# Output transform of a row-wise Winograd ResBlock: two-bank pairs through ScalarE to bf16, instead of f32 arithmetic on PSUM

## The chip, the cores and the metric

The kernel runs on one core of a Trainium2 chip. The metric is the device time of one execution in microseconds. The kernel before took 568.13, 567.94 and 566.29 us in three runs: median 567.94. One further execution was taken with the hardware profiler; every start and duration below is from it. The engines are TensorE (PE, with its weight loads as PEld), VectorE (DVE), ScalarE (ACT), GpSimd (POOL) and SyncE (SP), whose queue here issues nearly all DMA transfers. "L628" is line 628 of the kernel.

## The reference

The kernel computes one ResBlock of a diffusion model on bf16 tensors: batch 2, 512 channels, 64 x 64 pixels, four channel groups.

```
h = conv3(silu(gn(x, g1, be1)), w1)            # 3x3, padding 1
h = h + (silu(t_emb) @ w_emb).reshape(B, C, 1, 1)
h = conv3(silu(gn(h, g2, be2)), w2)
return x + h
# gn: per group of 128 channels: (z - mean) / sqrt(var + 1e-5) * gamma + beta
```

A channel group has 128 channels, which is just one tile of 128 partitions. The statistics of GroupNorm for a group need the sum and the sum of squares over a whole tile of 128 x 4096 values.

## The kernel before

**The convolution.** Each 3x3 convolution is done in a Winograd form along rows: four output rows are made from six transformed input rows. The six are called positions, 0 to 5. For each position, TensorE adds up products over 4 input channel tiles and 3 horizontal taps, so 12 matmuls of 128x128 weights by 512 columns (L628) fill one PSUM bank (128 x 512 f32). Six positions make a *set*: 72 matmuls, which give 32 output rows of 128 output channels. A *chunk* is one half image (32 rows) of one batch element, and has four sets, one for each output channel tile `ot`. There are four chunks in a layer and two layers: 32 sets and 2304 such matmuls.

**Around the matmuls, per set.** `evac(pos)` (L632 to L702) is called behind the matmuls of each position, in the order 1, 2, 3, 4, 0, 5. ScalarE copies positions 1 and 3 from PSUM to f32 tiles c1 and c3 with a factor 1/6 (L635, L649). VectorE combines positions 2 and 4 with them in f32, reading PSUM (L642, L654), so that t1 = p1 + p2 and t2 = p3 + p4 (scaled), and gets s1 = p1 - p2 and s2 = p3 - p4 by a multiply and subtract (L644, L656). The four output rows are then y1 = s1 + 2 s2, y2 = t1 + 4 t2, y0 = p0 + t1 + t2, y3 = p5 + s1 + 8 s2. In layer 0 (L661 to L667, L685, L693) four of these products also add up their own sums for the second GroupNorm, ScalarE squares the finished rows for the sum of squares (L697) into its own tile `junk`, and a DMA stores them to the scratch tensor h_scr (L699). In layer 1 (L669 to L681, L689, L701) the residual x, loaded as `xr`, is added by four more VectorE additions, and the result goes out (L702). There are 10 such VectorE operations per set in layer 0 and 14 in layer 1, each on 128 x 512 values with f32 on at least one side. PSUM holds six single-bank accumulators (pool `ps_acc`), and two further banks (`ps_x`) serve small products and transposes.

**Work beside it.** Three kinds of background tasks feed the matmuls:

- `produce_V` (L386) makes the transformed input V of the next chunk. For each of 4 input tiles: one load (from x in layer 0, from h_scr in layer 1), one ScalarE Silu with the GroupNorm's scale and bias (L415), and 14 VectorE operations in bf16 (L454 to L472). For the very first chunk, ScalarE does part of the scalings (L434 to L444).
- `prep_U` (L288) makes the transformed weights U of one output and one input tile: load of the weights (L290), nine TensorE transposes (L299, L302), two ScalarE copies from PSUM (L303, L305), and six VectorE operations (L328 to L336), of which three are fused multiply-adds through an f32 tile (L333, L334, L336). It runs 32 times; U of layer 0 is kept for both batch elements.
- `gn1_stats_bg` (L240) gets the first GroupNorm's statistics of batch element 1 while batch element 0 is convolved: for each of four channel tiles two loads (L245) into the pool `stg` under the tag "xr" (two buffers), ScalarE passes for the sum (L212) and the sum of squares (L216), and `gn_scale_bias` (L161): one small TensorE product over the partitions (L163), VectorE steps (L165 to L171, L180, L181) and two GpSimd steps (vare L173, rstd L178).

**What sets the order.** The class `_Background` (L19) keeps the tasks sorted by due time and counts in slots, one slot to a position. At each `bg.tick()` it adds credit at the highest rate that any due time needs, and runs a step of the most urgent task for each whole credit. In `evac`'s loop a tick comes before `evac(pos)`; in the very first set, whose matmuls go input tile by input tile as V comes in, it comes after. The order so written is then rearranged for each engine by the framework's scheduler, and every engine works its own list in order. The x loads of the statistics and of the residual are held back until the first set's first copy has been done (`first_evac`).

Of the kernel before, what the change touches and what calls it, by code (L numbers as in the profile page):

```python
# [10 lines left out]
ALU = mybir.AluOpType  # L11
# [52 lines left out]
def kernel(  # L64
# [32 lines left out]
    FAST_U = "s"  # L97
    ACT_TS0 = True
    N_SUM_ACT = 1
    RES_ON_PE = False  # L100
# [13 lines left out]
    otmp = ctx.enter_context(tc.tile_pool(name="otmp", bufs=1))  # L114
# [3 lines left out]
    ps_acc = ctx.enter_context(tc.tile_pool(name="ps_acc", bufs=6, space=PSUM))  # L118
# [169 lines left out]
    def prep_U(layer, ot, ct, eng=None, dep=None):  # L288
# [15 lines left out]
        g1t = wtmp.tile([P, NKX, P], BF16, tag="g1t")  # L304
        nc.scalar.copy(out=g1t[:], in_=pb[:])  # L305
        g0 = U[:, :, 0, :]
        g2 = U[:, :, NPOS - 1, :]
        if FAST_U == "both":
            g0q = wtmp.tile([P, NKX, P], BF16, tag="g0q")
            nc.scalar.activation(out=g0q[:], in_=pa[:, :, 0, :], func=ACT.Copy, scale=0.25)  # L310
            g1h = wtmp.tile([P, NKX, P], BF16, tag="g1h")
            nc.scalar.activation(out=g1h[:], in_=pb[:], func=ACT.Copy, scale=0.5)
            yield
            sb_ = wtmp.tile([P, NKX, P], BF16, tag="sb")
            nc.vector.tensor_tensor(out=sb_[:], in0=g0, in1=g2, op=ALU.add)
            nc.vector.tensor_tensor(out=U[:, :, 1, :], in0=sb_[:], in1=g1t[:], op=ALU.add)
            nc.vector.tensor_tensor(out=U[:, :, 2, :], in0=sb_[:], in1=g1t[:], op=ALU.subtract)
            yield
            cb_ = wtmp.tile([P, NKX, P], BF16, tag="sb")
            nc.vector.tensor_tensor(out=cb_[:], in0=g0q[:], in1=g2, op=ALU.add)  # L320
            nc.vector.tensor_tensor(out=U[:, :, 3, :], in0=cb_[:], in1=g1h[:], op=ALU.add)
            nc.vector.tensor_tensor(out=U[:, :, 4, :], in0=cb_[:], in1=g1h[:], op=ALU.subtract)
            yield
            return
        if FAST_U == "s":
            yield
            sb_ = wtmp.tile([P, NKX, P], BF16, tag="sb")
            nc.vector.tensor_tensor(out=sb_[:], in0=g0, in1=g2, op=ALU.add)  # L328
            nc.vector.tensor_tensor(out=U[:, :, 1, :], in0=sb_[:], in1=g1t[:], op=ALU.add)  # L329
# [28 lines left out]
    def emb_task():  # L358
# [5 lines left out]
        for i in range(EMB_NP):  # L364
# [13 lines left out]
            else:  # L378
                nc.vector.tensor_tensor(out=emb_sb[:], in0=emb_sb[:], in1=ps_e[:], op=ALU.add)
            yield  # L380

    POS_ORDER = (1, 2, 3, 4, 0, 5)
    Vt = {}
    V_STEPS = 3 * CT

# [377 lines left out]
```

## Time and profile before

| what | value |
|---|---|
| three runs | 568.13, 567.94, 566.29 us |
| profiled execution, span of its instructions | 564.7 us |
| profiled execution's own time, with what lies around the span | not shown on its page |
| TensorE busy | 540.7 us (96%) |
| VectorE busy | 479.8 us (85%) |
| ScalarE busy | 218.3 us (39%) |
| TensorE clock granted | 1.00 up to the last matmul |
| first main matmul starts, last one ends | 26.3 us, 558.7 us |

The same by stages, in us busy:

| stretch | what runs in it | TensorE | VectorE | ScalarE |
|---|---|---|---|---|
| 0 to 26.3 | loads, first statistics, first weights | 17.57 | 13.83 | 15.57 |
| 26.3 to 47.5 | first set | 17.48 | 18.55 | 19.37 |
| 47.5 to 101.1 | rest of the first chunk | 53.43 | 53.60 | 53.45 |
| 101.1 to 170 | second chunk | 65.87 | 64.47 | 28.65 |
| 170 to 266 | chunks 3 and 4, in part | 96.00 | 81.01 | 35.23 |
| 266 to 346.6 | end of layer 0, entry to layer 1 | 78.28 | 70.76 | 30.29 |
| 346.6 to 558.7 | layer 1 | 212.09 | 175.23 | 35.73 |
| 558.7 to 564.7 | tail | 0 | 2.30 | 0 |

How to read what follows. A group's row names line, engine, operation, output and inputs with their shape, then total busy time and the mean duration of one instruction in ns, then the idle time of the engine just before such instructions and what ended it. A row of the timeline has start and duration in us; idle time before it stands in brackets, with its releaser. A row of waits has total, number and longest. Neighbouring instructions of one engine overlap a little in the records, so the distance from start to start is shorter than the duration: a VectorE operation on 128 x 512 f32 values lasts 0.68 us and comes every 0.605 us.

### The profile page before, as it was taken

What the parts mean: (1) busy time and instruction counts of PE and PEld (TensorE: products, weight loads), DVE (VectorE), ACT (ScalarE), POOL (GpSimd) and SP (SyncE); (2) the same over time, 40 slices, a digit from 0 to 9 for tenths busy, and PEclk for the clock granted to TensorE, in tenths of its full rate; (3) what the DMA queues carried; (4) which work ended last, traced back from release to release, by engine and by line L of the source; (5) the groups of instructions that cost most, each with busy time, mean ns of one, the idle gap of its engine ahead of it and who ended that gap; (6) DMA issues with size and microseconds to landing.
All of it is one profiled execution on the core that took longest, in us unless ns stands there. A gap on an engine that the chain in (4) does not pass through costs nothing.

```text
span 564.7 us, 7699 instructions
## 1 busy us (share of the span) xinstructions
PE 540.7 (96%) x2814; PEld 259.3 (46%) x2814; DVE 479.8 (85%) x1226; ACT 218.3 (39%) x252; POOL 23.3 (4%) x74
## 2 busy tenths in 40 slices
PE   4879999899999999999999989999999999999995
PEld 4535544344444444444445545444444444444442
DVE  2889999989988884898879999999999998555665
ACT  5699999463435332343235314322230300000000
POOL 1110000011001100000000011000000000000000
PEclk9999999999999999999999999999999999999999
DMA  8506654333523120132133512323433122222210
GB/s 336 207 22 216 192 176 139 137 114 124 161 76 108 56 105 37 45 127 96 42 101 102 160 37 76 112 80 123 153 102 101 47 75 74 75 74 76 74 39 37
DMA packets 18754, 59.83 MB, mean 106 GB/s; under 512 B 2075, under 2 KB 3227, under 8 KB 18331
## 3 DMA queue, kind: packets, MB, share of 16 engines
q1 hardware_dynamic: 18656, 59.32, 31.5%
q8 instruction: 22, 0.36, 0.3%
q14 instruction: 17, 0.14, 0.1%
q10 hardware_dynamic: 59, 0.01, 0.0%
HBM read 42.54 MB, written 16.78 MB: 105 GB/s over the span
## 4 chain that ended last, share of the span: by engine, by line
PE 72%; DVE 21%; issue 2%; DMA 2%; ACT 1%; POOL 1%; SPq 0%; DVEq 0%; ACTq 0%
PE acc L628 70%; DVE U L336 2%; DVE U L334 2%; DVE U L329 1%; DMA xbuf<-in_x_dram 1%; DVE U L330 1%; POOL rstd L178 1%; DVE cc L333 1%; PE pa L299 1%; ACT V_146 L212 1%; DMA wn<-in_w_dram 1%; DVE vq L455 1%; DVE yst L662 1%; DVE tt L666 1%; DVE ss L667 0%
## 5 line engine op out<-in xcount | busy, mean ns | idle before, releaser
L628 PE MATMUL acc<-V,U 128*128 128x512 bf16 x2016 | 444.9, 381 | 2.6 <-DVE V L457 1.6
L628 PEld LDWEIGHTS <-U 128*128 128x128 bf16 x2304 | 224.0, 98 | 273.4 <-issue 7.0
L628 PE MATMUL acc<-V_146,U 128*128 128x512 bf16 x288 | 66.4, 381 | 3.2 <-DVE V_146 L448 3.1
L697 ACT ACTIVATE junk<-yst 128x2048 bf16<-128x2048 bf16 x16 | 30.5, 1909 | 58.5 <-DVE yst L693 53.2
L303 ACT COPY U<-pa 128x768 bf16<-128x768 bf16 x32 | 25.7, 803 | 41.1 <-PE pa L299 41.1
L415 ACT ACTIVATE a_tmp_105<-src,nb_all,sc_all 128x2112 bf16<-128x2112 bf16 x14 | 30.1, 2152 | 22.2 <-DVE V L470 18.9
L415 ACT ACTIVATE a_tmp_106<-src,nb_all,sc_all 128x2112 bf16<-128x2112 bf16 x14 | 30.1, 2151 | 21.5 <-DVE vq L455 10.4
L299 PEld LDWEIGHTS <-wn 128*128 128x128 bf16 x192 | 16.5, 142 | 8.0 <-issue 2.9
L299 PE MATMUL pa<-ident,wn 128*128 128x128 bf16 x192 | 16.9, 225 | 2.6 <-DVE tot L165 2.3
L334 DVE SCALAR_TENSOR_TENSOR U<-g1t,cc 128x384 bf16<-128x384 bf16 x32 | 17.5, 546 | 0.0
L333 DVE SCALAR_TENSOR_TENSOR cc<-U 128x384 f32<-128x384 bf16 x32 | 17.5, 546 | 0.0
L336 DVE SCALAR_TENSOR_TENSOR U<-g1t,cc 128x384 bf16<-128x384 bf16 x32 | 17.5, 546 | 0.0
L305 ACT COPY g1t<-pb 128x384 bf16<-128x384 bf16 x32 | 15.8, 495 | 0.4 <-DVE U L336 0.4
L216 ACT ACTIVATE xt<-xt 128x2048 bf16<-128x2048 bf16 x8 | 15.4, 1928 | 0.1
L212 ACT ACTIVATE xt<-xt 128x2048 bf16<-128x2048 bf16 x8 | 15.4, 1928 | 0.0
L199 PE MATMUL gr<-xbuf 128*128 128x128 bf16 x96 | 7.5, 243 | 6.5 <-DMA xbuf<-in_x_dram 6.5
L693 DVE SCALAR_TENSOR_TENSOR yst<-acc,ss 128x512 bf16<-128x512 f32 x16 | 10.9, 682 | 2.5 <-PE acc L628 2.5
L457 DVE TENSOR_TENSOR V<-vq 128x528 bf16<-128x528 bf16 x28 | 11.8, 422 | 0.0
L472 DVE TENSOR_TENSOR V<-V,vq 128x528 bf16<-128x528 bf16 x28 | 11.8, 421 | 0.0
L464 DVE TENSOR_TENSOR V<-vs,vq 128x528 bf16<-128x528 bf16 x28 | 11.8, 421 | 0.0
L466 DVE TENSOR_TENSOR V<-vs,vq 128x528 bf16<-128x528 bf16 x28 | 11.8, 421 | 0.0
L469 DVE TENSOR_TENSOR V<-V,vq 128x528 bf16<-128x528 bf16 x28 | 11.8, 421 | 0.0
(660 smaller groups left out, 594.6 us busy)
## 6 DMA issues: line engine op xcount, KB each, us to landing
wn<-in_w_dram SPq DMA_DIRECT2D x32, 288.0 KB, 3.1
src<-h_scr SPq DMA_DIRECT2D x16, 528.0 KB, 3.9
h_scr<-yst SPq DMA_DIRECT2D x16, 512.0 KB, 2.6
xr<-in_x_dram SPq DMA_DIRECT2D x16, 512.0 KB, 4.1
out_dram<-yst SPq DMA_DIRECT2D x16, 512.0 KB, 3.6
src<-in_x_dram SPq DMA_DIRECT2D x12, 528.0 KB, 4.5
xt<-in_x_dram SPq DMA_DIRECT2D x8, 512.0 KB, 3.7
xbuf<-in_x_dram SPq DMA_DIRECT2D x3, 1024.0 KB, 6.2
```

The source lines that it names most:

```text
L212: nc.scalar.activation(out=o, in_=pc, func=ACT.Identity, accum_out=part[:, k:k + 1])
L216: nc.scalar.activation(out=pc, in_=pc, func=ACT.Square, scale=float(HW) ** -0.5, accum_out=part[:, k:k + 1])
L299: nc.tensor.transpose(pa[:, kx, j, :], wn_v[:, kx, 2 * j, :], ident[:])
L303: nc.scalar.copy(out=U[:, :, 0:NPOS:NPOS - 1, :], in_=pa[:])
L305: nc.scalar.copy(out=g1t[:], in_=pb[:])
L333: nc.vector.scalar_tensor_tensor(out=cc[:], in0=g0, scalar=0.25, in1=g2, op0=ALU.mult, op1=ALU.add)
L334: nc.vector.scalar_tensor_tensor(out=U[:, :, 3, :], in0=g1t[:], scalar=0.5, in1=cc[:], op0=ALU.mult, op1=ALU.add)
L336: nc.vector.scalar_tensor_tensor(out=U[:, :, 4, :], in0=g1t[:], scalar=-0.5, in1=cc[:], op0=ALU.mult, op1=ALU.add)
L415: nc.scalar.activation(out=at[:, a_ - r0:b_ - r0, 1:W + 1], in_=ap, func=ACT.Silu, bias=nb_all[:, layer, b, ct:ct + 1], scale=sc_all[:, la ...
L457: nc.vector.tensor_tensor(out=Vc[:, 1], in0=p_, in1=q, op=ALU.add)
L628: nc.tensor.matmul(accs[pos][:], lhsT=U[ct][:, kx, pos, :], rhs=V[:, ct, pos, :, kx:kx + W], start=first, stop=last)
L697: nc.scalar.activation(out=junk[:], in_=yf, func=ACT.Square, scale=float(HW) ** -0.5, accum_out=ssq[:, ch:ch + 1])
```

## The change

The order of positions becomes 1, 3, 2, 4, 0, 5, and the accumulators are taken as three pairs, (1,3), (2,4) and (0,5), each one tile over two PSUM banks. `evac` runs once for a pair. ScalarE copies a whole pair (1024 values a partition) to a bf16 tile in one instruction; the pair (0,5) only in layer 1. VectorE then forms t1, t2 in one bf16 addition of 1024 values and s1, s2 in one subtraction, and the sums for y0 and y3 in one more. The fused multiply-adds for y1 and y2 in layer 1 become a scaling and an addition; the residual is added to the four rows at once, 2048 values, at the very end. In layer 0 the pair (0,5) is still read from PSUM by VectorE. The Square pass is put off to the first copy of the next set (`pending`, `flush_stats`), and its output goes to the tag "xr" that the statistics' loads also use. The temporaries have two buffers instead of one. `prep_U` goes from six VectorE operations to eight, all in bf16. In the first set two ticks come before each `evac`.

```diff
-    otmp = ctx.enter_context(tc.tile_pool(name="otmp", bufs=1))
+    otmp = ctx.enter_context(tc.tile_pool(name="otmp", bufs=2))
+    wpool = ctx.enter_context(tc.tile_pool(name="W", bufs=1))
-    ps_acc = ctx.enter_context(tc.tile_pool(name="ps_acc", bufs=6, space=PSUM))
+    ps_acc = ctx.enter_context(tc.tile_pool(name="ps_acc", bufs=3, space=PSUM))
...
-            cc = wtmp.tile([P, NKX, P], F32, tag="sc")
-            nc.vector.scalar_tensor_tensor(out=cc[:], in0=g0, scalar=0.25, in1=g2, op0=ALU.mult, op1=ALU.add)
-            nc.vector.scalar_tensor_tensor(out=U[:, :, 3, :], in0=g1t[:], scalar=0.5, in1=cc[:],
-                                           op0=ALU.mult, op1=ALU.add)
-            nc.vector.scalar_tensor_tensor(out=U[:, :, 4, :], in0=g1t[:], scalar=-0.5, in1=cc[:],
-                                           op0=ALU.mult, op1=ALU.add)
+        nc.vector.tensor_scalar(out=g1t[:, 1], in0=g1t[:, 0], scalar1=0.5, scalar2=None, op0=ALU.mult)
+        nc.vector.tensor_scalar(out=ev[:, 0], in0=g0, scalar1=0.25, scalar2=None, op0=ALU.mult)
+        nc.vector.tensor_tensor(out=ev[:, 1], in0=ev[:, 0], in1=g2, op=ALU.add)
+        nc.vector.tensor_tensor(out=U[:, :, 3, :], in0=ev[:, 1], in1=g1t[:, 1], op=ALU.add)
+        nc.vector.tensor_tensor(out=U[:, :, 4, :], in0=ev[:, 1], in1=g1t[:, 1], op=ALU.subtract)
...
-    POS_ORDER = (1, 2, 3, 4, 0, 5)
+    POS_ORDER = (1, 3, 2, 4, 0, 5)
...
+    pending = []
+
+    def flush_stats():
+        while pending:
+            yf, sq = pending.pop(0)
+            junk = stg.tile([P, CR * W], BF16, tag="xr")
+            nc.scalar.activation(out=junk[:], in_=yf, func=ACT.Square, scale=float(HW) ** -0.5, accum_out=sq)
...
                 def evac(pos):
+                    src = pairs[pos]
+                    if pos != 0 or layer == 1:
+                        m = otmp.tile([P, 2, TR, W], BF16, tag=f"m{pos}")
+                        i_a = nc.scalar.activation(out=m[:], in_=src[:], func=ACT.Copy,
+                                                   scale=KAPPA if pos != 0 else 1.0)
...
+                    if pos == 1:
+                        flush_stats()
                     elif pos == 2:
+                        w_ = wpool.tile([P, 2, 2, TR, W], BF16, tag="w")
+                        nc.vector.tensor_tensor(out=w_[:, :, 0], in0=tmp[1][:], in1=m[:], op=ALU.add)
+                        nc.vector.tensor_tensor(out=w_[:, :, 1], in0=tmp[1][:], in1=m[:], op=ALU.subtract)
+                        t1, s1, t2, s2 = w_[:, 0, 0], w_[:, 0, 1], w_[:, 1, 0], w_[:, 1, 1]
                         if layer == 0:
+                            nc.vector.scalar_tensor_tensor(out=y4[:, 1], in0=s2, scalar=2.0, in1=s1,
+                                                           op0=ALU.mult, op1=ALU.add, accum_out=acc_sum(0))
+                            nc.vector.scalar_tensor_tensor(out=y4[:, 2], in0=t2, scalar=4.0, in1=t1,
                                                            op0=ALU.mult, op1=ALU.add, accum_out=acc_sum(1))
                         else:
+                            sc2 = wpool.tile([P, 2, TR, W], BF16, tag="sc2")
+                            nc.vector.tensor_scalar(out=sc2[:, 0], in0=s2, scalar1=2.0, scalar2=None, op0=ALU.mult)
+                            nc.vector.tensor_scalar(out=sc2[:, 1], in0=t2, scalar1=4.0, scalar2=None, op0=ALU.mult)
+                            nc.vector.tensor_tensor(out=y4[:, 1], in0=sc2[:, 0], in1=s1, op=ALU.add)
+                            nc.vector.tensor_tensor(out=y4[:, 2], in0=sc2[:, 1], in1=t1, op=ALU.add)
+                        nc.vector.tensor_scalar(out=s2, in0=s2, scalar1=8.0, scalar2=None, op0=ALU.mult)
+                        nc.vector.tensor_tensor(out=w_[:, 0], in0=w_[:, 0], in1=w_[:, 1], op=ALU.add)
+                        tmp["w"] = w_
                     elif pos == 0:
                         yf = flat(yst)
                         if layer == 0:
+                            for i, f in enumerate((0, TH - 1)):
+                                nc.vector.scalar_tensor_tensor(
+                                    out=y4[:, f], in0=src[:, i], scalar=1.0, in1=tmp["w"][:, 0, i],
+                                    op0=ALU.mult, op1=ALU.add, accum_out=acc_sum(2 + i))
                             nc.sync.dma_start(out=h_scr[b, ot][:, rows], in_=yf)
+                            pending.append((yf, ssq[:, ch:ch + 1]))
                         else:
+                            nc.vector.tensor_tensor(out=y4[:, 0:TH:TH - 1], in0=m[:], in1=tmp["w"][:, 0], op=ALU.add)
+                            nc.vector.tensor_tensor(out=yf, in0=yf, in1=flat(xr), op=ALU.add)
                             nc.sync.dma_start(out=out_v[b, ot][:, rows], in_=yf)
...
                 if first_set:
...
-                    for pos in POS_ORDER:
-                        evac(pos)
-                        bg.tick()
+                    for pos in POS_ORDER[0::2]:
+                        bg.tick()
+                        bg.tick()
+                        evac(pos)
                 else:
...
                         bg.tick()
-                        evac(pos)
+                        if i % 2 == 1:
+                            evac(POS_ORDER[i - 1])
 
             if layer == 0 and ch == NCH - 1:
+                flush_stats()
```

The removed f32 forms of `evac` are those of the kernel before, shown above. Variants that were switched off (`FAST_U` other than "s", `RES_ON_PE`) are dropped as well.

## The prediction

> **What bounds the kernel now.** I read the busy table and the slices first, then the chain of work, then TensorE's waits, its timeline, and last the end of the run on VectorE. The busy table, the slices (tenths of 40 equal parts) and the chain:
>
> ```profile
> PE 540.7 (96%) x2814; PEld 259.3 (46%) x2814; DVE 479.8 (85%) x1226; ACT 218.3 (39%) x252; POOL 23.3 (4%) x74
> PE   4879999899999999999999989999999999999995
> DVE  2889999989988884898879999999999998555665
> ACT  5699999463435332343235314322230300000000
> PE 72%; DVE 21%; issue 2%; DMA 2%; ACT 1%; POOL 1%; SPq 0%; DVEq 0%; ACTq 0%
> ```
>
> TensorE is the bound at 96%. The change removes none of its matmuls. VectorE's 85% is an average: it is at 9 up to slice 34 and at 5 or 6 behind it. What lighter VectorE work can gain is therefore only what TensorE waits for it, and what comes behind the last matmul. TensorE's waits from 101 to 558 us (total, times, longest), and its timeline, in which bracketed idle time stands before a row:
>
> ```profile
> PE pa L299 <- DVE tot L165: 2.3, 1, 2.3
> PE acc L628 <- DVE V L457: 1.6, 1, 1.6
> PE acc L628 <- ACT c_1364 L635: 0.9, 1, 0.9
> PE ps L163 <- DVE me_1494 L224: 0.5, 1, 0.5
> ...
> 108.56 5.13 PE L628 MATMUL acc<-V,U 128*128 128x512 bf16 x22 [1.62 <-DVE V L457]
> ...
> 131.45 0.28 PE L163 MATMUL ps<-me_1562,ones_neg 128*128 128x2 f32 x2
> ...
> 338.94 0.53 PE L299 MATMUL pa<-ident,wn 128*128 128x128 bf16 x6 [2.32 <-DVE tot L165]
> ...
> 346.58 212.11 PE L628 MATMUL acc<-V,U 128*128 128x512 bf16 x972
> ```
>
> That is 5.3 us in all: 3.0 us while the second chunk runs (101 to 136), 2.3 us at the entry to layer 1. The last row runs 972 matmuls in 212.11 us without a gap: 0.218 us each, 15.7 us for a set of 72. VectorE's end, from the last set's fourth product on:
>
> ```profile
> 553.57 0.69 DVE L654 SCALAR_TENSOR_TENSOR t_5322<-acc,c_5308 128x512 f32<-128x512 f32 x1 [3.83 <-PE acc L628]
> ...
> 559.12 0.68 DVE L681 TENSOR_TENSOR yst<-t_5293,xr 128x512 bf16<-128x512 f32 x1
> 559.72 0.68 DVE L689 TENSOR_TENSOR yst<-acc,tt 128x512 bf16<-128x512 f32 x1
> 560.32 0.68 DVE L701 TENSOR_TENSOR yst<-acc,ss 128x512 bf16<-128x512 f32 x1
> ```
>
> The last matmul ends at 558.69, VectorE at 561.0, the store 3.7 us later at 564.7.
>
> **The change part by part.** The profiled span is 564.7 us; what lies around it is not shown, and the median 567.94 is 3.2 us more. I work out differences in the span and add them to the median.
>
> *VectorE per set.* The timeline's start-to-start steps, which pack tighter than the durations: 0.605 us for any 128x512 operation with f32; bf16 two-operand additions 0.27 at 384 elements, 0.345 at 528, 0.62 at 1056; bf16 scalings 0.205 at 528. I read from these 0.60 for 1024 and 1.14 for 2048. Layer 0: 10 x 0.605 = 6.05 becomes three additions of 1024, four 512 products with accumulation and one scaling: 7 x 0.60 + 0.20 = 4.4. Layer 1: 14 x 0.605 = 8.5 becomes four of 1024, two of 512 (0.34), three scalings and one of 2048: 2.4 + 0.7 + 0.6 + 1.14 = 4.8. Over 16 sets each that is -26 and -59 us.
>
> *Weight transform*, 32 times: three steps of 0.47 (rows of 0.55 us) become two scalings of 0.17 and three additions of 0.27: 1.41 to 1.15, -8 us. In all VectorE falls by about 93 us to 385. The bounds: if strided or scaled forms run at f32's pace, layer 0 stays at 6.0 and the fall is some 40.
>
> *ScalarE.* 64 copies of 512 (0.48 a step) become 80 of 1024. Between 512 and 768 elements (0.68) the step rises 0.20, so 1024 takes 0.89 to 0.91, with 1.03 busy: 31 to 73 us, +42, total 260 of 565. It is on the path in two places below. The PSUM pairs hold six banks as before; a pair comes free when ScalarE has copied it, or (0,5) in layer 0 when VectorE has added it, and is wanted two pairs (10.5 us) later: no wait while the copies are less than 9 us late.
>
> *Start of the run.* Compiled, the changed order has TensorE finish the first set near 44 instead of 47.5, but the weight transposes which before stood in that set's bubbles (31 to 38 us) then come behind it and wait for ScalarE's U copies (0.80) and for its Silu passes (2.15). By 58 us both have done the same. I take the first chunk's end at 101.6, against 101.1; bounds -1.5 and +2.
>
> *Second chunk.* The two V waits (1.6 + 0.9) go: V's additions finish about 13 us earlier. What is late next is batch 1's GroupNorm statistics. Before, its eight x loads (L245) issued from 45.5 us on; in the changed order all stand on SP's queue behind the h_scr store of the third set, and they share the two "xr" buffers with the Square pass, which formerly had its own. Third set: matmuls end at 101.6 - 15.7 = 85.9, and its last VectorE steps, behind V's additions in the queue, near 89.7; the load takes 3.7: 93.4. ScalarE then has, up to the fourth tile's last Square: 16 statistics passes x 1.89 = 30.2, four pair copies x 0.91 = 3.6, one deferred Square 1.9, two Silu x 2.05 = 4.1: 39.8, so 133.2, plus up to 1 us at each of three refills of the buffers (a 3.7 us load against 2.8 us of other work): 133.2 to 136.2, taken as 135.6, near the upper end because the refills stand behind stores on SP's queue. Each of the four statistics matmuls stands in TensorE's queue among the chunk's matmuls, the fourth after 141 of them, and everything behind it waits: weights, V products, the embedding matmuls. Before, 141 matmuls of that chunk were done at 136.4. So start and second chunk together give -0.8; ends: -3.0 + 0.5 = -2.5 when no statistic waits, and +4 when loads and handoffs are as slow as their slowest rows (8 x 0.3 on top of 136.2, and 2 for a later third set).
>
> *Entry to layer 1.* VectorE was behind there: between 330 and 339 it ran its f32 steps without pause, and tot came 2.3 us late. One chunk carries four sets x 3.7 fewer us, so its queue is empty when tot is due: -2.1, leaving 0.2 for the PSUM handoff; bounds -2.3 and 0.
>
> *The tail.* Behind the last pair (558.69) come one copy of 1024 (1.03), one addition of 1024 and one of 2048, each needing the one before, where dependent steps show 0.1 us more: 1.03 + 0.70 + 1.25 = 2.98 to the end of VectorE, against 561.0 - 558.7 = 2.3 before: +0.7. The earlier steps of that set (about 4.4 us from 553.45, plus a copy) are done before 559. Bounds: +0.3, and +2.2 if 1024 and 2048 take f32's pace.
>
> [...] The rows give 1.41 to 1.15 us for the weight transform although it goes from six operations to eight. [...] Batch 1's scalings stand on POOL: vare (L173) shows 190, 300 and 578 ns as lowest, median and highest, and VectorE waited for rstd 9.9 us in 15 times. [...]
>
> **Sum:** -0.8 - 2.1 + 0.7 = -2.2: span 562.5, time 565.7. Everywhere else VectorE's gain and ScalarE's loss count nothing, because matmuls run without a gap over both; a copy over 9 us late would end that cover and cost its excess.
>
> **The rivals.**
> - *A, as summed*: 565.7, spread 564.0 to 567.5.
> - *B, statistics don't bind.* The loads land early enough and ScalarE has slack (39% in all, but 9 in slices 3 to 6). Then -2.5 - 2.3 + 0.7 = -4.1: 563.8; with the first chunk's better end (-1.5) 561.8.
> - *C, slower: the statistics chain of batch 1 binds harder.* ScalarE is at 53.45 of 53.60 us busy between 47.5 and 101.1 already. The copies of four sets grow there by 8 x 0.43 = 3.4 us, and the late statistics free it only in part, so third set, loads and Squares may slide. Price: the fourth statistic's matmul at 141 instead of 135.6, so +5.4: 565.7 + 5.4 = 571.1 at worst, 570 at 140. It decides (time over 569.6) from 139.5 us on. Against it: the list above already holds every ScalarE operation that stands ahead of the fourth statistic.
> - *D, the change doesn't do what it says*: bf16 forms on strided pairs run one element a cycle, 1.14 for 1024. VectorE keeps its load in layer 0, the layer-1 entry stall stays (0), the tail gives +2.2, the second chunk -0.8: 569.3. Against it: 1056-element rows with both operands strided (L455) step 0.62.
>
> **How the numbers follow.** Three tenths of a per cent, 1.7 us, is about what a measurement of this kernel tells from no change (its runs spread 1.8): faster is below 566.2, slower above 569.6. Chances: A 0.50 (faster 0.28, same 0.20, slower 0.02), B 0.17 (faster), C 0.20 (slower 0.17, same 0.03), D 0.13 (slower 0.06, same 0.06, faster 0.01). Sums: 0.46, 0.29, 0.25. The range takes in B's lower end and C's worst: 561.8 to 571.5.
>
> **What would show it.** In the changed profile: VectorE busy near 385, ScalarE near 260; pair copies at 1.03 us, 1024 additions near 0.68 and the residual at 1.2; TensorE's idle rows between 101 and 136 naming statistics and not V; no gap near 339; the last VectorE row ending 3.0 us behind the last matmul. I am wrong if statistics matmuls wait more than 4 us in all, if the first chunk ends past 104, or if additions of 1024 take over 1 us.

## The result, and the profile after

The changed kernel is slower. It took 573.06, 574.40, 576.04 and 576.31 us, median 575.22, beside 567.12 for the kernel before on the same chip: ratio 1.0131, 95% interval 1.0103 to 1.0159. The forecast was 565.7, and its range ended at 571.5. The profiled execution took 576.31 us with a span of 574.5, so 1.8 us lie around the span.

The page of the changed kernel: busy table, slices of VectorE, ScalarE and TensorE's granted clock, the chain of work, and two groups (columns as before).

```profile
PE 545.6 (95%) x2811; PEld 260.7 (45%) x2814; DVE 398.0 (69%) x1194; ACT 263.4 (46%) x268; POOL 22.1 (4%) x74
DVE  2889999456968973698659999789634973223333
ACT  5898554899833452263355643344312511221121
PEclk9999999899999999999999998999999999999999
PE 69%; DVE 20%; ACT 5%; DMA 3%; issue 2%; POOL 1%; SPq 0%; ACTq 0%; DVEq 0%
L613 ACT ACTIVATE m<-acc 128x1024 bf16<-128x1024 f32 x80 | 81.3, 1018 | 176.9 <-PE acc L605 176.9
L650 DVE TENSOR_TENSOR yst<-yst,xr 128x2048 bf16<-128x2048 bf16 x16 | 19.5, 1221 | 0.3
```

VectorE fell from 479.8 to 398.0 us, as the change means it to, and the bound stayed where it was: TensorE. Its waits (total, times, longest):

```profile
PE ps L162 <- DVE me L223: 4.1, 3, 3.0
PE pa L298 <- ACT U L302: 2.9, 4, 1.6
PE pa L298 <- DVE tot L164: 2.0, 1, 2.0
PE acc L605 <- DVE V L404: 2.0, 1, 2.0
...
PE ps L162 <- DVE tot L164: 0.8, 2, 0.4
```

The first row is batch 1's GroupNorm statistics in the second chunk; the second is the weight transposes of the first chunk; the third is the entry to layer 1, where before stood 2.3 us. Where the rows lie, from TensorE's timeline:

```profile
107.35 0.38 PE L162 MATMUL ps<-me,ones_neg 128*128 128x2 f32 x2 [3.01 <-DVE me L223]
...
141.80 0.38 PE L162 MATMUL ps<-me,ones_neg 128*128 128x2 f32 x2 [0.49 <-DVE me L223]
...
343.46 0.53 PE L298 MATMUL pa<-ident,wn 128*128 128x128 bf16 x6 [1.97 <-DVE tot L164]
...
355.63 212.11 PE L605 MATMUL acc<-V,U 128*128 128x512 bf16 x972
```

The last row is the same 212.11 us for 972 matmuls as before, begun 9.05 us later: the whole loss lies ahead of it, but for the tail. A ledger of the sets shows in which stage. It gives the start of a set's first matmul (L628 before, L605 after).

| set | before | after | later by | what lies between the rows |
|---|---|---|---|---|
| 0 | 26.31 | 27.31 | 1.0 | start |
| 2 | 68.61 | 71.50 | 2.9 | first two sets |
| 4 | 101.10 | 103.97 | 2.9 | rest of the first chunk |
| 5 | 120.12 | 125.06 | 4.9 | first set of the second chunk |
| 7 | 153.69 | 159.54 | 5.8 | two more sets |
| 17 | 316.60 | 322.61 | 6.0 | chunks 3 and 4 |
| 19 | 354.43 | 363.48 | 9.05 | entry to layer 1 |
| end of the last | 558.32 | 567.36 | 9.05 | layer 1 |

So first chunk +2.9, second +3.0, chunks 3 and 4 +0.2, entry to layer 1 +3.0, and +0.7 behind the last matmul: 9.8, the difference of the spans (574.5 - 564.7).

Two of these stages lost more than they waited. The second chunk waited 4.1 us against 3.0 before, yet fell back 3.0; the entry waited 3.1 (1.97 + 0.36 + 0.41 + 0.33) against 2.3, and fell back 3.0. Most of the rest, 1.7 of 1.9 us and 1.7 of 2.2, is the granted clock. In the trace's record of it the clock is 0.5 for 3.41 us from 108.82 and again from 344.34, just behind the two long waits; half speed for 3.41 us costs 1.7 us (run 5 measures 1.68). Windows of the changed kernel (busy time of each engine, granted clock, DMA share, GB/s; the first window of the entry stands for comparison):

```profile
110.00:120.00 10.00, 10.00 (x43) 4.23 (x41) 0.81 (x4) 8.90 (x10) 0.60 (x2) 0.89 0.27 91
...
330.00:340.00 10.00, 9.23 (x53) 4.82 (x52) 9.28 (x34) 2.34 (x4) 1.26 (x3) 1.00 0.38 106
340.00:350.00 10.00, 7.70 (x41) 3.87 (x40) 8.19 (x37) 4.91 (x5) 2.58 (x6) 0.83 0.17 55
...
360.00:370.00 10.00, 10.00 (x47) 4.50 (x46) 9.10 (x23) 4.08 (x3) 0.15 (x1) 1.00 0.14 43
```

From 110 to 120 TensorE is busy throughout and gets through 43 instructions; from 360 to 370, where nearly all are matmuls of 512 columns as well and the clock is 1.00, it gets through 47.

Why the statistics come late is on SyncE's queue and ScalarE. SyncE's queue after, and the same load before:

```profile
92.64 0.34 SPq L646 DMA_DIRECT2D h_scr<-yst  x1
93.03 13.84 SPq L244 DMA_DIRECT2D xt<-in_x_dram  x4
```

```profile
45.52 1.01 SPq L245 DMA_DIRECT2D xt<-in_x_dram  x2
```

The loads moved from 45.5 to 93.0 us, behind the third set's store. ScalarE's timeline then shows the first statistic's chain, and its neighbours:

```profile
97.46 1.91 ACT L211 ACTIVATE xt<-xt 128x2048 bf16<-128x2048 bf16 x1 [1.91 <-DMA xt<-in_x_dram]
...
104.53 1.90 ACT L215 ACTIVATE xt<-xt 128x2048 bf16<-128x2048 bf16 x1
106.33 0.19 ACT L215 ACTIVATION_READ_ACCUMULATOR xt<-xt 128x1 f32 x1
107.45 1.91 ACT L211 ACTIVATE xt<-xt 128x2048 bf16<-128x2048 bf16 x1 [0.93 <-DMA xt<-in_x_dram]
```

The last pass ends at 106.5, and the product of the statistics, which TensorE has reached at 104.34, runs at 107.35.

### The profile page after: what moved, and what is told of

Its sections match the earlier page's. It is cut to its first block, busy times and chain, and to the rows that moved or that the text cites. A ratio compares the mean times of both kernels' runs of the same rounds, so it can differ in the third digit from the quotient of the medians.

```text
span 574.5 us, 7661 instructions
## 1 busy us (share of the span) xinstructions
PE 545.6 (95%) x2811; PEld 260.7 (45%) x2814; DVE 398.0 (69%) x1194; ACT 263.4 (46%) x268; POOL 22.1 (4%) x74
## 4 chain that ended last, share of the span: by engine, by line
PE 69%; DVE 20%; ACT 5%; DMA 3%; issue 2%; POOL 1%; SPq 0%; ACTq 0%; DVEq 0%
PE acc L605 67%; DMA xt<-in_x_dram 2%; ACT xt L215 1%; ACT xt L211 1%; DVE U L310 1%; DVE U L317 1%; DVE U L311 1%; DVE ev L315 1%; DVE ev L309 1%; DVE U L316 1%; DVE ev L314 1%; DMA xbuf<-in_x_dram 1%; DVE yst L643 1%; ACT a_tmp L381 1%; DVE g1t L313 1%
## 5 line engine op out<-in xcount | busy, mean ns | idle before, releaser
L605 PE MATMUL acc<-V,U 128*128 128x512 bf16 x2304 | 513.1, 383 | 2.7 <-DVE V L404 2.0
L605 PEld LDWEIGHTS <-U 128*128 128x128 bf16 x2304 | 225.0, 99 | 273.0 <-issue 6.7
L613 ACT ACTIVATE m<-acc 128x1024 bf16<-128x1024 f32 x80 | 81.3, 1018 | 176.9 <-PE acc L605 176.9
L381 ACT ACTIVATE a_tmp<-src,nb_all,sc_all 128x2112 bf16<-128x2112 bf16 x28 | 60.0, 2149 | 38.4 <-DVE V L436 18.5
L650 DVE TENSOR_TENSOR yst<-yst,xr 128x2048 bf16<-128x2048 bf16 x16 | 19.5, 1221 | 0.3
L421 DVE TENSOR_TENSOR vq<-vq,a_tmp 128x1056 bf16<-128x1056 bf16 x28 | 19.6, 701 | 0.2
L425 DVE TENSOR_TENSOR vs<-a_tmp 128x1056 bf16<-128x1056 bf16 x28 | 19.5, 698 | 0.0
L423 DVE TENSOR_TENSOR V<-vq 128x528 bf16<-128x528 bf16 x28 | 11.9, 426 | 1.8 <-PE acc L605 1.7
L420 DVE TENSOR_SCALAR vq<-a_tmp 128x1056 bf16<-128x1056 bf16 x28 | 11.9, 426 | 0.6 <-ACT a_tmp L381 0.4
L438 DVE TENSOR_TENSOR V<-V,vq 128x528 bf16<-128x528 bf16 x28 | 11.9, 424 | 0.1
L424 DVE TENSOR_TENSOR V<-vq 128x528 bf16<-128x528 bf16 x28 | 11.9, 424 | 0.0
L436 DVE TENSOR_TENSOR V<-a_tmp 128x528 bf16<-128x528 bf16 x28 | 11.9, 424 | 0.0
```

The costliest lines, as they stand in the source:

```text
L381: nc.scalar.activation(out=at[:, a_ - r0:b_ - r0, 1:W + 1], in_=ap, func=ACT.Silu, bias=nb_all[:, layer, b, ct:ct + 1], scale=sc_all[:, la ...
L421: nc.vector.tensor_tensor(out=vqf, in0=vqf, in1=rows2(3), op=ALU.subtract)
L425: nc.vector.tensor_tensor(out=vsf, in0=rows2(3), in1=rows2(1), op=ALU.subtract)
L605: nc.tensor.matmul(accs[pos], lhsT=U[ct][:, kx, pos, :], rhs=V[:, ct, pos, :, kx:kx + W], start=first, stop=last)
L613: i_a = nc.scalar.activation(out=m[:], in_=src[:], func=ACT.Copy, scale=KAPPA if pos != 0 else 1.0)
L650: nc.vector.tensor_tensor(out=yf, in0=yf, in1=flat(xr), op=ALU.add)
```

## The experiments

Theory A: the arithmetic does what the forecast said, and the loss is one of order. The new order and the shared buffer tag bring three small waits on TensorE, two of which pull the clock down. The rivals, in turn: the eight-step weight transform costs the loss (B in the run `old_U`), the engines are short of time so that a removed wait only moves, and the clock has nothing to do with the waits. All edits are against the changed kernel unless something else is said, and all compute the whole reference.

**1. Squares with their own buffer.** The Square pass gets a tile of its own, so that the statistics' loads no longer share "xr" with it; the copies of positions 1 and 3 give back one buffer to make room.

```diff
-            junk = stg.tile([P, CR * W], BF16, tag="xr")
+            junk = wpool.tile([P, CR * W], BF16, tag="sc2")
-                        m = otmp.tile([P, 2, TR, W], BF16, tag=f"m{pos}")
+                        m = otmp.tile([P, 2, TR, W], BF16, tag=f"m{pos}", bufs=1 if pos == 0 else 2)
```

> The Square pass writes to a buffer of its own again, so the statistics' loads of batch 1 have the two xr buffers to themselves; all else is the changed kernel (m0 has one buffer for space). Theory A, the shared buffers hold the loads back: the loads L244 issue from about 46 us on instead of 93.0, the statistics matmuls of the second chunk wait 0 to 1 us instead of 4.1, its half-clock stretch (3.41 us, 1.7 us lost) is gone, and the set that starts at 175.24 us starts 3 to 6 us earlier; time 569.5 to 572.5 against 575.2 of the changed kernel. Part may be lost again in the first chunk, where ScalarE then has 30 us of statistics passes more. Rival B, the longer ScalarE copies are what delays the statistics: waits stay over 3 us, time 574 to 576.

580.32 us (578.41 to 581.98), ratio 1.0223 [1.0192, 1.0254]: slower still. The cause it was made for is right. SyncE's queue now has the loads at 48.7 us, the waits for statistics are gone from the list, and the first set of the second chunk takes 15.84 us (108.74 to 124.58) where the changed kernel took 21.09. But one wait came and one grew (from 2.9 us in all), both through ScalarE's queue:

```profile
PE ps_e L338 <- ACT s_sb L328: 5.4, 1, 5.4
PE pa L298 <- ACT U L302: 3.8, 4, 1.9
```

The second one: with loads this early, ScalarE meets the statistics' passes among the weight copies of the first chunk, and stands for a load in front of a copy that TensorE wants.

```profile
54.88 1.91 ACT L211 ACTIVATE xt<-xt 128x2048 bf16<-128x2048 bf16 x1 [2.05 <-DMA xt<-in_x_dram]
56.70 0.19 ACT L211 ACTIVATION_READ_ACCUMULATOR xt<-xt 128x1 f32 x1
56.79 0.78 ACT L302 COPY U<-pa 128x768 bf16<-128x768 bf16 x1
```

Set 2 starts at 76.1, 4.6 us later than in the changed kernel; 1.7 of that, an estimate from a half clock's 3.41 us, goes to one in the first set (nine matmuls from 31.43 take 3.12 us, and 2.12 from 30.75 in the changed kernel). The first one: the embedding's small Silu (s_sb) stands in ScalarE's queue behind V's normalizations, one of which waited 2.80 us for its source. TensorE stood 5.41 us up to 146.34, and the clock was 0.5 for 6.83 us about there (eight matmuls from 146.77 take 3.57 us). So A is right on what holds the statistics and wrong on the time: the wait moved.

**2. The weight transform as before.** The three fused multiply-adds through f32 instead of five bf16 operations.

```diff
-        nc.vector.tensor_scalar(out=g1t[:, 1], in0=g1t[:, 0], scalar1=0.5, scalar2=None, op0=ALU.mult)
...
+        cc = wtmp.tile([P, NKX, P], F32, tag="sc")
+        nc.vector.scalar_tensor_tensor(out=cc[:], in0=g0, scalar=0.25, in1=g2, op0=ALU.mult, op1=ALU.add)
...
```

> The weight transform goes back to three fused operations on VectorE; all else is the changed kernel. Theory A, the weight transform plays no part: time within 0.7 us of the changed kernel's 575.2, the third set starting at 71.5 us as there. Rival B, its eight operations and their later results cost the first chunk: the third set starts 1 to 2 us earlier, time 573 to 574.5.

575.69 us (573.45 to 576.88), ratio 1.0138 [1.0112, 1.0165]: the changed kernel's 1.0131 within the intervals, so the time is A's, to some 1.5 us. The sign that A named did not come: the third set starts at 74.48, not at 71.5, because in this profiled execution the first main matmul starts at 31.10 instead of 27.31. From there to the third set it takes 43.4 us, and 44.2 in the changed kernel. A difference under 1 us between the two forms is therefore not ruled out.

**3. The second batch's statistics of layer 1 due later.** The second GroupNorm's task for batch 1 gets a due time two sets later (24 slots for 12); nobody needs it before layer 1's third chunk.

```diff
-                                  slot_of(0, idx, CT - 1) + SLOTS + 2 * SLOTS)
+                                  slot_of(0, idx, CT - 1) + SLOTS + (2 if b == 0 else 4) * SLOTS)
```

> The second GroupNorm's statistics of batch 1 are due two sets later (after the last weight transposes); all else is the changed kernel. Theory A, at the entry to layer 1 four statistics in a bunch hold the two small PSUM banks until VectorE copies them, and the transposes behind them wait: the waits of 0.36, 0.41, 1.97 and 0.33 us near 338 to 344 and the half-clock stretch at 344.3 go, 3 to 4.8 us; time 570.5 to 572.5. Rival B, VectorE is behind there whatever comes: a wait of 2 us or more comes back at the next transposes, time 574 or more.

569.73 us (568.99 to 572.24), ratio 1.0047 [1.0025, 1.007]. The waits at the entry are gone, and nothing took their place. TensorE's whole list between the start and the end, in the second chunk and behind it, is now the statistics and nothing else:

```profile
PE ps L162 <- DVE me L223: 4.2, 3, 3.2
```

By the ratios, 0.8 of the loss of 1.3% went by one due time. The time is 0.8 us under what A expected. The profile shows no half clock in the second chunk either, though TensorE waited 3.15 us up to 108.18 (47 matmuls from 108.42 take 10.41 us); that saving of 1.7 us is not the edit's, as the wait there is no shorter than the changed kernel's 3.01 (last section). Windows of the two kernels, changed first, show that VectorE is no less busy for it (third busy figure):

```profile
320.00:330.00 10.00, 10.00 (x61) 5.17 (x59) 10.00 (x31) 4.75 (x7) 0.00 (x0) 1.00 0.43 140
```

```profile
330.00:340.00 10.00, 10.00 (x67) 5.51 (x66) 10.00 (x33) 3.99 (x6) 0.16 (x1) 1.00 0.30 96
340.00:350.00 10.00, 10.00 (x61) 5.13 (x59) 10.00 (x30) 4.76 (x8) 0.00 (x0) 1.00 0.27 77
```

VectorE is full ahead of the place of the wait in either kernel (up to 330 in the changed one, up to 350 here), with the weights of layer 1, V and the output transform. What the edit does is to take out of it a chain that TensorE waits for.

**4. The same due time in the kernel before.**

```diff
-                                  slot_of(0, idx, CT - 1) + SLOTS + 2 * SLOTS)
+                                  slot_of(0, idx, CT - 1) + SLOTS + (2 if b == 0 else 4) * SLOTS)
```

> The kernel before, with the one edit that the second GroupNorm's statistics of batch 1 are due two sets later; its f32 transform stays. Theory A, the wait at the entry to layer 1 comes from four statistics in a bunch that hold the two small PSUM banks, whatever VectorE's load: the wait of 2.32 us near 339 goes, time 565.0 to 566.0 against 567.8. Rival B, it is VectorE's backlog of f32 work, as the prediction had it: a wait of 1.5 us or more stays at the last weight transposes, time 567.3 to 568.3.

568.6 us (568.5 to 569.36), ratio 1.0022 [1.0013, 1.0032]. The wait of 2.32 us went and came back some 36 us later:

```profile
374.98 0.38 PE L163 MATMUL ps<-me,ones_neg 128*128 128x2 f32 x2 [3.00 <-DVE tot L165]
...
379.81 0.38 PE L163 MATMUL ps<-me,ones_neg 128*128 128x2 f32 x2 [1.37 <-DVE me L272]
```

VectorE's row for that copy of tot, behind one set's f32 additions:

```profile
374.18 0.68 DVE L681 TENSOR_TENSOR yst<-t,xr 128x512 bf16<-128x512 f32 x1
374.78 0.21 DVE L165 COPY tot<-ps 128x2 f32<-128x2 f32 x2
```

So A missed: it held the due time to be as good for either kernel. B had the backlog right, but neither the place of the wait nor the time, which is 0.3 us over its range. From 350 to 370 VectorE is busy for 20.00 of 20 us here, and for 13.46 in run 3. In this pair of runs the later due time pays only with the lighter VectorE work.

**5. Gaps made on purpose.** To price the clock by itself: in layer 1, where TensorE runs without a gap, five sets begin with 1, 3, 5, 8 and 12 ScalarE copies that the set's first matmul waits for (added to the changed kernel).

```diff
+    GAPS = {(1, 1, 1): 1, (1, 1, 3): 3, (1, 2, 1): 5, (1, 2, 3): 8, (1, 3, 1): 12}
...
+                for k in range(GAPS.get((layer, idx, ot), 0)):
+                    gt = ps_x.tile([P, NFREE], F32, tag="x", name="gt")
+                    gap = nc.scalar.activation(out=gt[:], in_=flat2(gap_src[0], k), func=ACT.Copy, scale=1.0)
```

> Five deliberate waits of TensorE are put into layer 1 of the changed kernel: the first matmuls of five sets wait for 1, 3, 5, 8 and 12 ScalarE copies into an unused PSUM bank, for gaps of about 1.7, 2.6, 3.6, 5.0 and 7.0 us; nothing is left out. Theory A, a wait of TensorE itself brings the half clock: the gaps of 3.6 and more are each followed by 3.41 us at clock 0.5 (1.7 us lost), those of 1.7 and 2.6 by none; span about 574.5 + 19.9 + 3 x 1.7 = 599.5. Rival B, the half-clock stretches of the changed kernel have another cause (the load on the chip, the start of a chunk): no stretch behind the new gaps, span about 594.4.

608.52 us in one run. TensorE's timeline, 144 matmuls behind each of the first four gaps:

```profile
400.37 33.25 PE L615 MATMUL acc<-V,U 128*128 128x512 bf16 x144 [3.86 <-ACT gt L612]
436.46 31.57 PE L615 MATMUL acc<-V,U 128*128 128x512 bf16 x144 [2.84 <-ACT gt L612]
471.92 33.24 PE L615 MATMUL acc<-V,U 128*128 128x512 bf16 x144 [3.88 <-ACT gt L612]
510.59 32.97 PE L615 MATMUL acc<-V,U 128*128 128x512 bf16 x144 [5.43 <-ACT gt L612]
```

And the clock in windows of the same run (granted clock third from the end):

```profile
436.50:439.90 3.40, 3.40 (x16) 1.54 (x17) 0.22 (x1) 0.00 (x0) 0.00 (x0) 1.00 0.66 228
400.83:404.24 3.41, 3.41 (x10) 1.17 (x9) 3.31 (x7) 0.84 (x1) 0.00 (x0) 0.50 0.57 214
```

A gap of 3.86 us costs 1.68 us on top of itself (33.25 - 31.57); behind the one of 2.84 us the clock stayed at 1.00. Half clocks follow four of the five gaps (the last is 7.50 us), so rival B falls. The gaps came out longer than planned, so what A says of short ones isn't tested by them. The waits of the other runs do that, below.

**6. The first chunk.** Gram matrix and column sums of the first statistics share one two-bank tile, as a free pair may be what they wait for, and two of the next chunk's source loads are held to the first set's first copy, so that their normalizations don't stand in front of weight copies.

```diff
-        gr = pool.tile([P, NFREE], F32, tag=tag, name="gr")
+        st = ps_acc.tile([P, 2, NFREE], F32, tag="acc", name="gr")
...
+                if (layer, b, ch) == (0, 0, 1) and ct < 2:
+                    after(i_d, first_evac[0] if first_evac else None)
```

> The changed kernel with two edits before and in its first set: Gram and column sums of one channel tile share one two-bank tile, and the first two x loads for the next chunk's V wait for the first pair copy, so that ScalarE's two Silu passes at 41 to 45 us no longer stand ahead of the weight copies. Theory A, the first chunk's loss of 2.9 us is the pairs' doubled PSUM tiles (1.0 us before the first matmul) and ScalarE's order (1.9 us): first main matmul near 26.3 instead of 27.3, third set at 69.0 to 70.5 instead of 71.5, time 572.5 to 574.5. Rival B, the longer copies themselves: both stay within 0.5 us, time 575 to 576.

575.39 us (574.6 to 575.82), ratio 1.0132 [1.0117, 1.0147]: nothing. Set 2 starts at 71.52, as in the changed kernel (71.50), the first main matmul at 27.82 (27.31), and the wait behind the column sums (1.15 us) stays, so the shared tile didn't remove it. A missed. The time is B's, but a time within B's range doesn't show that the longer copies are the cause. The run is of use for the clock. Its entry to layer 1 has the changed kernel's waits, 1.98 and 0.33 us, and no half clock: the twelve matmuls behind them take 2.78 us from 344.46, and in the changed kernel 4.33 from 344.58.

**7. Own buffer, and the embedding's Silu at the start.** Run 1, with the transpose and the Silu of the embedding moved to the first statistics, out of ScalarE's queue in the second chunk.

```diff
+    def emb_silu():
+        ps_t = ps_x.tile([P, B * ET], BF16, tag="x")
...
+            emb_silu()
```

> The Square pass has its own buffer, as before, and the embedding's transpose and Silu are done at the very start; all else is the changed kernel. Theory A, with early statistics only the embedding's Silu stood in the way, behind three Silu passes that wait for the next V: the wait of 5.41 us and the 6.83 us at half clock behind it go, no wait over 1 us between 105 and 170, time 570 to 573 against 580.3. Rival B, ScalarE's queue is late anyway: the wait comes back at another matmul, time 576 or more.

579.55 us (578.73 to 582.03), ratio 1.0214 [1.0188, 1.024]. That is B: the wait moved again, to VectorE's additions of the embedding's partial sums, which stand behind the output transform and hold the PSUM buffer:

```profile
147.26 0.35 PE L341 MATMUL ps_e<-s_sb,wt 128*128 128x2 bf16 x8 [3.87 <-DVE emb_sb L346]
```

**8. All four edits of order together** (runs 1, 3, 6 and 7).

> All four repairs in the changed kernel: own buffer for the Square pass, embedding's Silu at the start, later due time of the second GroupNorm's statistics, one tile for Gram and column sums with held V loads. Theory A, the arithmetic of the change costs only the tail's 0.6 us, and what it lost came from order: time 563.5 to 567, at or under the kernel before (567.8). Rival B, the arithmetic itself (ScalarE's 45 us more) costs more than 1 us: 568.5 or more.

567.84 us (566.69 to 568.2), ratio 1.0003 [0.9991, 1.0016]: level with the kernel before, 0.8 us over the upper end of what A gave and 0.7 under the lower end of B's. The arithmetic is that of the changed kernel, so the 1.3% were the order's. Set 2 starts at 71.70 instead of run 1's 76.1; 1.7 us of that are put down to the half clock of run 1, and the rest went with the edits of run 6 (idle by themselves) and run 7. There is no half clock before the end. What is left in TensorE's list beside the first chunk is the wait of run 7, shorter:

```profile
PE ps_e L339 <- DVE emb_sb L344: 1.9, 1, 1.9
```

**9 and 10. The embedding's sums elsewhere.** Both add one edit to run 8: ScalarE copies the four partial sums out of PSUM, and VectorE adds them later; or the embedding's task runs in the first chunk.

```diff
-            if i == 0:
-                nc.vector.tensor_copy(out=emb_sb[:], in_=ps_e[:])
+            nc.scalar.copy(out=emb_p[:, i], in_=ps_e[:])
```

> The version with all four edits of order, plus one: the four partial sums of the embedding are copied out of PSUM by ScalarE, and VectorE adds them afterwards. In that version TensorE waited 1.93 and 0.37 us for VectorE's copies of them, because they stood behind the additions of the output transform in VectorE's queue (L344 at 141.41 us). Theory A (what is left is order alone, and nothing else is hidden behind this wait): the two waits go, ScalarE is idle for 3.4 us there, no half clock; 2.3 us less than 567.8, that is 565.0 to 566.5. Theory B (the whole set is short of VectorE or ScalarE, so that the wait moves once more, to the statistics, the V rows or the pair copies): 567.3 to 569.

566.43 us (566.16 to 567.15), ratio 0.9991 [0.9982, 1.0], at the upper end of A: 0.8 us of the wait stays, and the fourth load of the embedding's weights is now late by 1.57 us.

```diff
-                if layer == 0 and idx == 1 and ot == 0:
-                    t_emb_task = bg.add(emb_task(), EMB_STEPS, slot_of(0, 1, CT - 1))
+                if layer == 0 and idx == 0 and ot == 2:
+                    t_emb_task = bg.add(emb_task(), EMB_STEPS, slot_of(0, 1, 0))
```

> The version with all four edits of order, plus one: the embedding's matmuls and sums are put into the third and fourth sets of the first chunk (due at its end), instead of the second chunk. Theory A (VectorE has room there, the second chunk's wait of 2.3 us goes and nothing else comes): 565.0 to 566.5. Theory B (the embedding's weight loads and its two PSUM buffers now stand between the weight transforms of the first chunk's last set, and the wait moves to the U copies there): 567.5 to 570.

568.2 us (566.78 to 568.54), ratio 1.0016 [1.0004, 1.0027]. B's number, but not by B's mechanism: the wait is again that for a statistic, 1.92 us in front of a product at 102.05, with slow matmuls behind it (ten from 102.30 take 3.37 us, and 2.34 at full clock in run 1).

**11. The embedding's weights loaded by GpSimd's queue.** Run 9, and the four loads leave SyncE's queue, where they stood behind source loads.

```diff
-            nc.sync.dma_start(out=wt[:, 0:n, :], in_=wemb_v[:, e0:e0 + n, :])
+            nc.gpsimd.dma_start(out=wt[:, 0:n, :], in_=wemb_v[:, e0:e0 + n, :])
```

> The version with five edits (the embedding's sums copied by ScalarE), plus one: the four loads of the embedding's weights are issued by GpSimd, not on SyncE's queue. With five edits TensorE still waited 0.77 us for a copy and 1.57 us for the fourth of these loads (SyncE issued a load at 140.61, and stood for 9.32 us before it on three source loads). Theory A (the load was only held in SyncE's queue): the 1.57 us go, 564.3 to 565.6 where the version before it took 566.4. Theory B (the load waits for a staging buffer, whoever issues it, or the wait moves again): 566.0 to 567.5.

564.65 us (564.47 to 565.07), beside 566.44 for the kernel before: ratio 0.9956 [0.9941, 0.997]. A holds. This version beats both kernels: the first by 0.4%, the changed one by some 10 us. That the change of arithmetic is what wins the 0.4% isn't shown: of the edits of order only the due time was tried on the kernel before (run 4). That kernel's own waits between 101 and 558 us are 5.3 us for V, a copy, a statistic and tot, none of them for the embedding. Its busy table and its waits behind the first chunk:

```profile
PE 541.4 (96%) x2814; PEld 260.6 (46%) x2814; DVE 397.0 (70%) x1193; ACT 262.6 (47%) x273; POOL 24.4 (4%) x79
```

```profile
PE ps_e L340 <- ACT emb_p L344: 0.9, 1, 0.9
```

The work on each engine is that of the changed kernel; the span is 563.3 instead of 574.5 us. Its third set still starts 3.2 us later than that of the kernel before (71.76 against 68.61), so the first chunk's loss is not settled.

## Why the prediction was wrong

The sum said -2.2 us in the span, and +9.8 came: a miss of 12.0. By its own terms:

| term | predicted | measured | miss |
|---|---|---|---|
| first chunk | +0.5 | +2.9 | 2.4 |
| second chunk | -1.3 | +3.0 | 4.3 |
| chunks 3 and 4 | 0 | +0.2 | 0.2 |
| entry to layer 1 | -2.1 | +3.0 | 5.1 |
| tail | +0.7 | +0.7 | 0 |

**What held.** Every price of an instruction: the pair copy lasts 1.018 us (1.03 given), the addition of 1024 0.69 (0.68), the residual 1.22 (1.2); VectorE's sum is 398 us (385, so 13 too low), ScalarE's 263 (260); VectorE ends 3.0 us behind the last matmul (2.98). The two V waits of the second chunk are gone. GpSimd's vare didn't get longer (median 246 ns, 300 before). Rival D, that the bf16 forms don't run fast, falls by these rows. The weight transform in more operations cost no time that run 2 could tell from nothing, to some 1.5 us. It lies beside matmuls, so no run here prices the number of operations on a path that counts. Two of the three signs of error that the forecast named came true or nearly: the statistics' matmuls waited 4.1 us in all, over 4, and the first chunk ended at 103.97, just short of 104. The forecast's "no gap near 339" did not come: TensorE waited 1.97 us up to 343.46.

**"By 58 us both have done the same."** This step failed. The place was right: the weight transposes of the second set stood for ScalarE's U copies. But there was no catching up: the first main matmul starts 1.0 us later than before (27.31 for 26.31), the first set takes 21.76 us in both kernels, and the second 22.43 instead of 20.54, which makes 2.9. In the second set TensorE's idle time is 1.07 us instead of 0.17, nearly all of it waits for U copies (0.24 and 0.69); its other 1.0 us is more busy time. What delays the start, and these copies, stays open; run 6 tried one account of it and moved nothing.

**The fourth statistic's matmul, "taken as 135.6".** The mechanism was right, in the forecast and in its rival C: the loads stand behind the shared "xr" buffers, shown by run 1. The size was off. The loads began at 93.0 for 89.7, as the chunk was late and the store with it, a load took 4.5 us from issue to landing (3.7 before), and the fourth matmul came at 141.80. C put its price at the fourth statistic: +5.4 us if that ran at 141. That is not where the time went: the fourth matmul waited 0.49 us, the first 3.01. C was right on the direction and not on the place. The working timed only the last of four products. Each stands at its own place in TensorE's queue, and the first is reached at 104.34, 0.4 us into the chunk, where the lateness of the loads is felt whole. The first product's wait could have been had from the forecast's own numbers: a load landed at 93.4, and four passes of 1.89, a Square of 1.9 and a pair copy of 0.91 behind it, end at 103.8; the queue is at that product at 101.6 + 0.4 = 102.0.

**"Its queue is empty when tot is due."** This failed, and it was the largest term. The working counts four sets of layer 1 at 3.7 us less each, but by 339 only two (their first matmuls at 298.78 and 316.60) had gone through; the sets ahead of them belong to layer 0 and lose 1.65 us each by the forecast's own figures. Nor does such a saving empty a queue in a stretch that is full for another reason: VectorE is at 10.00 of 10.00 us from 310 to 330 in the changed kernel too. And part of the delay was no backlog at all. The forecast read that VectorE ran between 330 and 339 "without pause"; its rows in the kernel before say otherwise:

```profile
331.92 0.16 DVE L180 TENSOR_TENSOR sc_all<-rstd,gb 128x1 f32<-128x1 f32 x1 [0.35 <-POOL rstd L178]
...
333.46 0.16 DVE L180 TENSOR_TENSOR sc_all<-rstd,gb 128x1 f32<-128x1 f32 x1 [0.59 <-POOL rstd L178]
```

VectorE's rows in the changed kernel, in front of the wait:

```profile
338.44 0.68 DVE L622 TENSOR_TENSOR w__3393<-m 128x1024 bf16<-128x1024 bf16 x1
339.84 0.16 DVE L179 TENSOR_TENSOR sc_all<-rstd,gb 128x1 f32<-128x1 f32 x1 [0.72 <-POOL rstd L177]
...
341.64 0.16 DVE L179 TENSOR_TENSOR sc_all<-rstd,gb 128x1 f32<-128x1 f32 x1 [0.58 <-POOL rstd L177]
...
343.25 0.15 DVE L164 COPY tot<-ps 128x2 f32<-128x2 f32 x1
```

VectorE stands twice for GpSimd's rstd of the earlier tiles and works a whole pair's output transform before it copies tot; TensorE's next transposes want the PSUM buffer that this copy frees. It is the place of a chain in an in-order queue, and run 3 shows it: with a later due time the 3.0 us go while VectorE stays full. Run 4 shows that the load counts too, but as a condition: the same due time in the kernel before gains nothing, since there the wait returns.

**What was in no term: the clock.** Two half clocks of 3.41 us cost 1.7 us each, 3.4 of the 12.0. The kernel before has its own wait of 2.32 us and no half clock, so no row of it behind the first main matmul shows the price. Its three times, though, fall into two groups (566.29 against 567.94 and 568.13), and the step between them is about one half clock (last section).

**The base.** The sum was put on the median of 567.94, as what lies around the span wasn't known. With 1.8 us around it, the profiled execution of before was near 566.5: 1.4 us below the median. From there the same sum would have given 564.3, so this fault made the miss smaller.

## What to carry to other kernels

When the bounding engine works an in-order queue, price a change by the place of each of its waits in that queue, and for each product that is delayed time the first one, not the last. A buffer tag shared between a pass and a load is an edge in the order (run 1: without it the loads go out at 48.7 us instead of 93.0): ask what the load now stands behind on its DMA queue. When one removed wait comes back elsewhere, follow it through the queues (here ScalarE's Silu, VectorE's partial sums, SyncE's loads): the gain came only with the sixth edit of order, on arithmetic that was the same from the start.

## What the runs showed of the hardware

**The clock drops behind some waits of TensorE, and not behind others as long.** In the changed kernel it is 0.50 from 108.82 to 112.24 and from 344.34 to 347.76; in run 5 from 400.83 to 404.24, 472.51 to 475.92 and 510.06 to 513.47, at gaps of 3.86, 3.88 and 5.43 us, and from 547.61 to 554.43 at that of 7.50. In run 7 slow matmuls show it behind the 3.87 us: twelve from 148.20 take 5.11 us, and 2.78 at full clock. The length of a wait doesn't decide it alone in these rows. One of 1.97 us in the first set stands in several runs, and the nine matmuls behind it take 3.12 us in run 1 and 3.42 in run 5, but 2.12 in the changed kernel and in runs 3 and 7. The wait of 3.01 us in the changed kernel brought a half clock; that of 3.15 us in run 3, the gap of 2.84 us in run 5 and the 2.32 us of the kernel before brought none. What decides it was not shown. Run 6 against the changed kernel prices it at equal waits: behind 1.98 and 0.33 us twelve matmuls take 2.78 us, behind 1.97 and 0.33 the same twelve take 4.33, so 1.55 us lie between them. The same wait costs some 1.6 us in one profile and nothing in another. The kernel before has two groups of times that fit this: of its 62 executions taken beside runs 1 to 11, 30 took 566.26 to 566.93 us at a mean granted clock of 0.998 or 0.999, and 32 took 567.69 to 568.72 at 0.995 or 0.996, with none between; 0.003 of 565 us is 1.7 us, as much as one half clock. Which of the two comes up more often moves its median from 566.44 (beside run 11) to 567.77 (beside run 8), so ratios from different measurements can differ by 0.2% for this reason alone. That the clock also makes the spread of the changed kernel's runs (573.06 us at 0.996, the others up to 576.31 at 0.990 to 0.993) fits, but was only argued.

**An idle edit is not a useless one.** The held source loads of run 6 gave nothing by themselves, and with early statistics loads set 2 started at 71.70 (run 8) instead of 75.11 (run 7, where 1.7 us is put down to a half clock: six matmuls from 57.17 take 2.52 us, and 1.47 from 66.32). Run 8 differs from run 7 by the later due time as well, whose gain in run 3 lies at the entry to layer 1. Edits of order don't add up.
